# Coarse and fine exponents of an S4D unit in one product, with half of the coarse factors multiplied on GpSimd

## The chip, the cores and the metric

The kernel runs on one core of a Trainium2 chip. Its five engines have instruction streams of their own and meet through semaphores: PE (TensorE, matrix products into PSUM; PEld are its weight loads), DVE (VectorE), ACT (ScalarE, table functions and copies), POOL (GpSimd) and SP (SyncE, which issues nearly all DMAs here). The metric is the time of one execution on the device, in microseconds (us); lower is better.

## The reference

Two branches over the same length of 2048 positions and 640 channels are mixed by a gate:

```
dt = exp(log_dt);  A = -exp(log_A_real) + 1j*A_imag;  C = (C_real + 1j*C_imag) * dt
P = exp((A*dt)[:, :, None] * pos)                  # 640 channels x 128 states x 2048 positions
K = 2 * Re(einsum("dn,dnl->dl", C, P))             # taps: one filter of 2048 per channel
a = irfft(rfft(u, 4096) * rfft(K, 4096))[:2048] + u * D_skip
b = relu(x @ w1) @ w2                              # FFN, 640 -> 1728 -> 640
g = sigmoid((u * gate_w).sum(-1))
out = g * a + (1 - g) * b
```

The taps K are the part that the change touches. Position l is split into a coarse and a fine part, 64 coarse slots of 32 fine positions each. The complex exponential is then a product of a coarse and a fine factor, and the sum over the 128 states is a matrix product of the two.

## The kernel before

**Stages.** Three bodies of work are interleaved on the same engines. (1) The FFN: fp32 operands split into a high and a low part, three matmuls per product, in three passes over the hidden size (5, 5 and 4 blocks of 128). Its PSUM tile is pf. It has no dependence on the rest until the end, and fills PE wherever there is room. (2) The generation of the taps: 40 units of 16 channels (`products`, `factors`), joined in 20 pairs (`taps`). (3) The convolution by a two-stage transform, in 5 blocks of 128 channels (`conv`, PSUM tile pc). It opens when the last taps are in DRAM, since it reuses the memory of the generation.

**A unit.** `params` leaves eight rows per channel, high and low parts of the phase and magnitude parameters, in DRAM; `load_rows` fetches them as `R[c]`, 128 rows for 16 channels with the states along the columns. `products` (line 1166) multiplies them on PE by constant tables in `tg`. Two PSUM tiles result: pg, from four matmuls that each use a 32-row tile of PE (four channels, 512 columns: per channel 64 phases, 32 fine and 32 coarse, and 64 exponents of coarse factors), and pe, from one matmul over all 128 rows (16 channels x 32 exponents of fine factors). ACT rounds the phases to integers into sc (`whole`), takes the exponential of the coarse exponents into mg and of the fine ones into me (`exps`). DVE subtracts the integers from the phases (`part`, from PSUM and sc) and masks off the sign for the cosine. ACT takes sine and cosine of both.

**Factors.** `factors` (line 1213) makes, on DVE, the coarse sine factors G in two halves (the sine changes sign between the halves, which is why the 64 coarse slots stand in the order 32..63, 31..0, function `slots`), then mg times the cosine in place, then both fine factors times me. `taps` sums over the states on PE: 128 matmuls a unit pair and operand (mg and G against sc) into pk. DVE transposes pk to kt, POOL adds the skip term (an add of 128x8), and four DMAs store kt to kd. The convolution loads kd as ck.

**What sets the order.** Every piece of work is a task with an engine, an estimated duration, dependencies, buffer tokens from rings (pg, pe, pk have one buffer, mg four, sc five) and a rank. `Plan.run` plays the tasks against these estimates and emits the instructions engine by engine in the order in which it picks them. On the chip, each engine runs its stream in that fixed order. `moves` (line 135) adds a correction to the rank of single tasks by number. `Plan.add` with `port=True` charges a DVE task a quarter of the time in which POOL is taken by the estimates. All instructions are recorded through one helper, so the profile names one line for nearly all of them, and groups are told apart by tile names.

Short names used below: the subtraction is `sc<-pg,sc` on DVE, the masking `sc<-sc` on DVE, the cast `sc<-pg` on ACT, the exponential `mg<-pg` on ACT.

Of the kernel before, what the change touches and what calls it, by code (L numbers as in the profile page):

```python
# [46 lines left out]
TGR = 6  # L47
TGA = 4
# [26 lines left out]
def tables():  # L75
# [20 lines left out]
    tg = np.zeros((16, 8, 180))  # L96
    tg[:, :2, :32], tg[:, :2, 32:64], tg[:, 2:4, :32] = b, 32 * b + 16, 1
    tg[:, 4:6, 64:128], tg[:, 4:6, 128:160], tg[:, 6:, 128:160] = 32 * slots(), b, 1
    tg[np.arange(16), :, 160 + np.arange(16)] = 1
    tg[np.arange(16), :, 176 + np.arange(16) % 4] = 1  # L100
    f = lambda x: np.ascontiguousarray(x.astype(np.float32))
    return dict(t_g=f(tg.reshape(128, 180)), t_f1=f(np.tile(np.stack([f1, f1[slots()]], axis=1), (2, 1, 1))), t_w=f(w.reshape(128, 64)),
# [32 lines left out]
def moves():  # L135
    r = {}
    for v, s in (
# [318 lines left out]
class Kernel:  # L456
# [519 lines left out]
    def params(self):  # L976
# [116 lines left out]
        def steps_in():  # L1093
            tl['tgs'] = self.prm.tile([128, 180], F32, name="tgs")
            D_.dma_start(tl['tgs'], io['t_g'])
# [520 lines left out]
```

## Time and profile before

| | us |
|---|---|
| median of 3 runs (663.16 to 666.48) | 663.31 |
| profiled execution, its own time | 662.23 |
| span of that execution, first to last instruction | 660.5 |
| busy PE / DVE / ACT / POOL | 621.1 / 536.0 / 398.8 / 91.4 |

The span is cut into 40 slices of 16.5 us. Each digit of a slice is the busy share of an engine in tenths. Matmul records overlap in the pipe, so PE's busy share overstates how full it is; the distance between two starts says more. In the rows of groups, the columns are: operation, output<-inputs, shape, count | busy us, mean ns of one | idle time of the engine just before them and what ended it. In the rows of a timeline: start in us from the span's start, duration in us, engine, operation. A row of waits has the total, the count and the longest wait in us. The generation of taps lies between 87 us, when the first product of a unit runs, and 404 us, when the last pair is transposed; the convolution follows to the end.

### The profile page before, as it was taken

To read this page: it belongs to the slowest core of one execution; us is meant where nothing else is said; L and a number is where in the kernel's file an instruction comes from. 1 tells how busy PE (TensorE), PEld (TensorE's weight loads), DVE (VectorE), ACT (ScalarE), POOL (GpSimd) and SP (SyncE) were. 2 spreads that over 40 slices of the span, in tenths; PEclk is the share of its full clock that TensorE was granted. 3 is DMA by queue.
4 is the path that set the end of the run, shared out by engine and by line. 5 is a ranking of instruction groups with operands and counts; after the bars stand their busy time and mean duration, and the time that the engine had idled before them with its cause. 6 is when DMAs were issued, how large, how long until landed. Compare 5 with 4: busy or idle time off the path is not lost.

```text
span 660.5 us, 19174 instructions
## 1 busy us (share of the span) xinstructions
PE 621.1 (94%) x8236; PEld 486.3 (74%) x8236; DVE 536.0 (81%) x778; ACT 398.8 (60%) x591; POOL 91.4 (14%) x133
## 2 busy tenths in 40 slices
PE   7999999899999999999998998999888999998996
PEld 6999988797988978878876977655663445754666
DVE  4799939989999999988998994879568677977642
ACT  5447369999999888778798891032334342432631
POOL 0000000000000000000000000033051170612741
PEclk9999999999999999999998997999989999999999
DMA  9956675142555533425441363964515847336535
GB/s 243 328 190 195 195 221 176 25 162 81 171 169 187 211 121 122 169 97 192 150 119 39 109 165 123 331 191 82 212 39 151 199 124 161 130 100 168 144 104 129
DMA packets 76302, 102.79 MB, mean 156 GB/s; under 512 B 7609, under 2 KB 59449, under 8 KB 75962
## 3 DMA queue, kind: packets, MB, share of 16 engines
q1 hardware_dynamic: 76058, 101.16, 50.9%
q8 instruction: 65, 1.06, 0.7%
q10 hardware_dynamic: 160, 0.41, 0.2%
q14 instruction: 19, 0.16, 0.1%
HBM read 62.36 MB, written 39.19 MB: 154 GB/s over the span
## 4 chain that ended last, share of the span: by engine, by line
PE 66%; DVE 10%; issue 8%; DMA 6%; ACT 5%; SPq 2%; POOL 2%; POOLq 0%; DVEq 0%; ACTq 0%
PE pf L434 44%; PE pc L434 13%; PE pk L434 6%; PE pg L434 2%; DMA ck<-kd 2%; SPq L434 2%; DVE sc L434 2%; ACT sc L434 2%; DVE G L434 2%; DMA out_dram<-yo 2%; DMA xu<-in_A_u_dram 2%; PE pe L434 1%; POOL ku L434 1%; DVE mg L434 1%; ACT mg L434 1%
## 5 line engine op out<-in xcount | busy, mean ns | idle before, releaser
L434 PE MATMUL pf<-xx,w1h 128*128 128x256 f32 (+1 forms) x760 | 189.0, 346 | 1.5 <-DVE hl L434 0.9
L434 PEld LDWEIGHTS pf<-xx,w1h 128*128 128x128 f32 x760 | 125.1, 192 | 34.3 <-issue 21.1
L434 PE MATMUL pf<-xx,w1l 128*128 128x512 f32 (+1 forms) x340 | 116.5, 343 | 0.1
L434 DVE STREAM_TRANSPOSE ku<-pc 128x512 f32<-128x512 f32 x80 | 77.9, 1062 | 19.5 <-PE pc L434 19.4
L434 PE MATMUL pf<-w2h,hh 128*128 128x320 f32 x288 | 90.2, 317 | 2.5 <-DVE q L434 1.6
L434 PE MATMUL pf<-w2l,hh 128*128 128x320 f32 x288 | 88.1, 310 | 0.0
L434 ACT COPY ku<-pc 128x512 f32<-128x512 f32 (+1 forms) x60 | 43.8, 751 | 54.9 <-PE pc L434 54.9
L434 PE MATMUL pf<-w2h,hl 128*128 128x320 f32 x256 | 75.0, 317 | 0.0
L434 PEld LDWEIGHTS pf<-xx,w1l 128*128 128x128 f32 x340 | 65.1, 192 | 8.0 <-DVE w1l L434 0.3
L434 POOL TENSOR_TENSOR ku<-ku,kx 128x256 f32<-128x256 f32 x80 | 55.8, 735 | 97.8 <-DVE ku L434 34.9
L434 POOL TENSOR_TENSOR kt<-kt,dsk 128x8 f32<-128x8 f32 x20 | 8.4, 420 | 394.4 <-DVE kt L434 394.4
L434 ACT CAST sc<-pg 128x1024 int32<-128x1024 f32 x40 | 40.4, 1010 | 36.5 <-PE pg L434 36.5
L434 PEld LDWEIGHTS pf<-w2h,hh 128*128 128x128 f32 x288 | 54.3, 189 | 10.1 <-issue 4.9
L434 DVE TENSOR_TENSOR sc<-pg,sc 128x1024 f32<-128x1024 f32 x40 | 48.8, 1220 | 14.8 <-ACT mg L434 14.5
L434 PEld LDWEIGHTS pf<-w2l,hh 128*128 128x128 f32 x288 | 54.4, 189 | 0.2
L434 ACT ACT_TABLE_LOAD x42 | 53.9, 1283 | 0.7
L434 PEld LDWEIGHTS pf<-w2h,hl 128*128 128x128 f32 x256 | 46.5, 188 | 9.3 <-issue 9.3
L434 DVE TENSOR_TENSOR mg<-mg,sc 128x1024 f32<-128x1024 f32 x40 | 48.9, 1223 | 2.5
L434 DVE TENSOR_TENSOR sc<-sc,me 128x1024 f32<-128x1024 f32 x40 | 48.7, 1218 | 0.0
L434 ACT ACTIVATE hh<-pf 128x512 fp32r<-128x512 f32 (+1 forms) x40 | 20.4, 510 | 43.6 <-PE pf L434 43.4
L434 ACT ACTIVATE sc<-sc,half_pi 128x1024 f32<-128x1024 f32 x40 | 45.7, 1143 | 0.0
L434 PE MATMUL pk<-mg,sc 128*32 128x64 f32 x1280 | 39.8, 226 | 4.7 <-DVE sc L434 3.4
(166 smaller groups left out, 1197.2 us busy)
## 6 DMA issues: line engine op xcount, KB each, us to landing
xx<-xt SPq DMA_DIRECT2D x24, 640.0 KB, 7.7
xt<-xx SPq DMA_DIRECT2D x16, 640.0 KB, 6.3
part<-q SPq DMA_DIRECT2D x16, 640.0 KB, 3.3
q<-part SPq DMA_DIRECT2D x16, 640.0 KB, 4.6
ws<-in_B_w_dram SPq DMA_DIRECT2D x20, 320.0 KB, 3.5
kd<-kt SPq DMA_DIRECT2D x80, 64.0 KB, 1.7
ck<-kd SPq DMA_DIRECT2D x40, 128.0 KB, 3.6
xu<-in_A_u_dram SPq DMA_DIRECT2D x10, 512.0 KB, 7.7
```

The costliest lines, as they stand in the source:

```text
L434: return lambda *a, **k: self._tc.keep_in_program_order(f(*a, **k))
```

## The change

The fine exponents move into the 32-row tiles. Per channel a tile has 128 columns: 32 fine phases, 32 coarse phases, 32 coarse exponents (slots 32 down to 1) and 32 fine exponents. The matmul into pe is gone (the PSUM tile pe is left for the transposes at the start), and one exponential per unit covers coarse and fine exponents, 1024 elements a partition as the old coarse one did. It writes into a tile mg with 98 columns a channel. The upper 32 coarse factors are no longer exponentials: POOL multiplies the 32 computed ones, read backwards, by the factor of slot 31, into the first 32 columns, and sets the factor of slot 0 to 1. The factors on DVE read and write the same numbers of elements as before, at the new pitch. The table `t_g` shrinks from 180 to 132 columns and is scaled into `tg` by four ACT instructions in place of 20. The two halves of the coarse operand in `taps` stand apart in memory by 33 columns. The corrections in `moves` are replaced throughout, so that all five engines' orders are new.

```diff
-                q = st['pe', c] = self.psg.tile([128, 2, 256], F32, name="pe").rearrange("p a (d j) -> p (a d) j", j=32)
-                self.E.matmul(q.rearrange("p d j -> p (d j)"), R[c], self.tg[:, 512:], start=True, stop=True)
                 p = self.psg.tile([128, 8, 256], F32, name="pg").rearrange("p (r x) n -> p r (x n)", x=2)
                 for r in range(4):
                     x = slice(32 * r, 32 * r + 32)
-                    self.E.matmul(p[:, r], R[c][x], self.tg[x, :512], start=True, stop=True)
+                    self.E.matmul(p[:, r], R[c][x], self.tg[x], start=True, stop=True)
...
-            def exps(k):
-                def go():
-                    if k:
-                        st['mg', c] = st['gp'].tile([128, C, 64], F32, name="mg", bufs=4)
-                        S.activation(st['mg', c].rearrange("p (r e) j -> p r e j", e=4), st.pop(('px', c)), AF.Exp)
-                    else:
-                        st['me', c] = st['gp'].tile([128, C, 32], F32, name="me", bufs=4)
-                        S.activation(st['me', c], st.pop(('pe', c)), AF.Exp)
-                return go
+            def exps():
+                m = st['mg', c] = st['gp'].tile([128, C, 98], F32, name="mg", bufs=4)
+                S.activation(m[:, :, 32:].rearrange("p d (x j) -> p d x j", x=2)[:, :, :, :32], st.pop(('px', c)), AF.Exp)
+
+            def long():
+                m = st['mg', c]
+                P.memset(m[:, :, 64:65], 1.0)
+                P.tensor_mul(m[:, :, :32], m[:, :, 63:31:-1], m[:, :, 33:34].to_broadcast([128, C, 32]))
...
-            y = acts[c, 2] = A('ACT', None, 0.52, exps(0), [a, x], use=[e_, m_], rank=2, mode='exp')
-            d = A('DVE', 'g1', 1.14, part, [b, x], use=[p_, s_], rank=G1R)
+            d = A('DVE', 'g1', 1.14, lambda: V.tensor_sub(st['sc', c][0], st.pop(('pg', c)), I(st['sc', c][1])), [b, x],
+                  use=[p_, s_], rank=G1R)
+            y = A('POOL', 'm', 1.6, long, [x], use=[m_], rank=1)
...
-            tasks[c] = dict(s=s_, m=m_, exps=[x, y], trig=[sn, cs])
+            tasks[c] = dict(s=s_, m=m_, exps=[y, x], trig=[sn, cs])
...
-                        m = mg.rearrange("p d (h j) -> p d h j", h=2)
-                        V.tensor_mul(m, m, cs[:, :, None, 32:].to_broadcast([128, C, 2, 32]))
+                        V.tensor_mul(mg, mg, cs[:, :, None, 32:].to_broadcast([128, C, 2, 32]))
                     else:
                         x = st.pop(('s2', c))[:, :, :, :32]
-                        V.tensor_mul(x, x, me[:, None].to_broadcast([128, 2, C, 32]))
+                        V.tensor_mul(x, x, m[:, None, :, 65:97].to_broadcast([128, 2, C, 32]))
...
```

Left out of the diff are the two lists of `moves`, the host tables, the scaling of `tg`, views of the same tiles, and the list by which `ssm` puts ACT's tasks of a pair in line, which loses the second exponential.

More of the change, by code (lines that the diff above doesn't have):

```diff
@@ L93, in tables @@
             n[g % 4, :, g // 4, p, 1] = np.stack([sk, ck], axis=1)
[L96 to L100, printed above, removed]
+    tg = np.zeros((16, 8, 132))
+    tg[:, :2, :32], tg[:, :2, 32:64], tg[:, 2:4, :64] = b, 32 * b + 16, np.repeat([1, 0], 32)
+    tg[:, 4:6, 64:96], tg[:, 4:6, 96:128], tg[:, 6:, 96:128] = 32 * (32 - b), b, 1
+    tg[np.arange(16), :, 128 + np.arange(16) % 4] = 1
     f = lambda x: np.ascontiguousarray(x.astype(np.float32))
-    return dict(t_g=f(tg.reshape(128, 180)), t_f1=f(np.tile(np.stack([f1, f1[slots()]], axis=1), (2, 1, 1))), t_w=f(w.reshape(128, 64)),
+    return dict(t_g=f(tg.reshape(128, 132)), t_f1=f(np.tile(np.stack([f1, f1[slots()]], axis=1), (2, 1, 1))), t_w=f(w.reshape(128, 64)),
                 t_m=f(m.reshape(128, 32, 64)), t_n=f(n.reshape(128, 8, 2, 2, 64)))
@@ L1093, in steps_in @@
         def steps_in():
-            tl['tgs'] = self.prm.tile([128, 180], F32, name="tgs")
+            tl['tgs'] = self.prm.tile([128, 132], F32, name="tgs")
             D_.dma_start(tl['tgs'], io['t_g'])
@@ L1098, in go @@
             def go():
-                a, b = self.tg[:, :512].rearrange("p (x e j) -> p e x j", x=2, j=64), self.tg[:, 512:].rearrange("p (d j) -> p d j", j=32)
                 for d in ds:
-                    S.mul(b[:, d], tl['tgs'][:, 128:160], tl['tgs'][:, 160 + d:161 + d])
-                    if d % 4 == 0:
-                        S.mul(a[:, d // 4], tl['tgs'][:, :128].rearrange("p (x j) -> p x j", x=2),
-                              tl['tgs'][:, 176 + d // 4:177 + d // 4])
+                    S.mul(self.tg[:, d * 128:d * 128 + 128], tl['tgs'][:, :128], tl['tgs'][:, 128 + d:129 + d])
             return go
-        a = A('SP', 'tg', 0.62, steps_in, [self.prm0], kb=88, rank=TGR)
+        a = A('SP', 'tg', 0.62, steps_in, [self.prm0], kb=66, rank=TGR)
         if TGR > 5:
             self.late_loads.append(a)
-        for d in range(0, 16, 4):
-            self.tg_done.append(A('ACT', 'tg', 1.3, spread(range(d, d + 4)), [a], rank=TGA))
+        for d in range(0, 4, 2):
+            self.tg_done.append(A('ACT', 'tg', 0.7, spread(range(d, d + 2)), [a], rank=TGA))
         return [*done, *self.tg_done]
@@ L1123, in ssm @@
         self.gw = gk.tile([128, D], F32, name="gw")
-        self.tg = gk.tile([128, 1024], F32R, name="tg")
+        self.tg = gk.tile([128, 512], F32R, name="tg")
         dsk = gk.tile([128, n // 2, 2 * Q], F32, name="dsk")
@@ L1166, in products @@
         def products(c):
-            p_, e_, s_, m_ = tok('pg'), tok('pe'), tok('sc'), tok('mg')
+            p_, s_, m_ = tok('pg'), tok('sc'), tok('mg')
             rd, r_ = rows[c]
             def pe():
-                q = st['pe', c] = self.psg.tile([128, 2, 256], F32, name="pe").rearrange("p a (d j) -> p (a d) j", j=32)
-                self.E.matmul(q.rearrange("p d j -> p (d j)"), R[c], self.tg[:, 512:], start=True, stop=True)
                 p = self.psg.tile([128, 8, 256], F32, name="pg").rearrange("p (r x) n -> p r (x n)", x=2)
@@ L1175, in pe @@
                     x = slice(32 * r, 32 * r + 32)
-                    self.E.matmul(p[:, r], R[c][x], self.tg[x, :512], start=True, stop=True)
-                p = p.rearrange("p r (x e j) -> p x r e j", x=2, j=64)
-                st['pg', c], st['px', c] = p[:, 0], p[:, 1]
+                    self.E.matmul(p[:, r], R[c][x], self.tg[x], start=True, stop=True)
+                p = p.rearrange("p r (e j) -> p (r e) j", j=128)
+                st['pg', c], st['px', c] = p[:, :, :64], p[:, :, 64:].rearrange("p d (x j) -> p d x j", x=2)
             def whole():
@@ L1182, in whole @@
                 st['sc', c] = [st['s2', c][:, k] for k in range(2)]
-                S.copy(I(st['sc', c][1]).rearrange("p (r e) j -> p r e j", e=4), st['pg', c])
-            def exps(k):
-                def go():
-                    if k:
-                        st['mg', c] = st['gp'].tile([128, C, 64], F32, name="mg", bufs=4)
-                        S.activation(st['mg', c].rearrange("p (r e) j -> p r e j", e=4), st.pop(('px', c)), AF.Exp)
-                    else:
-                        st['me', c] = st['gp'].tile([128, C, 32], F32, name="me", bufs=4)
-                        S.activation(st['me', c], st.pop(('pe', c)), AF.Exp)
-                return go
@@ L1195, in part @@
-            def part():
-                x, y = (t.rearrange("p (r e) j -> p r e j", e=4) for t in st['sc', c])
-                V.tensor_sub(x, st.pop(('pg', c)), I(y))
-            a = visit[c] = A('PE', None, 0.5, pe, [rd, opened, *self.tg_done], take=[p_, e_], use=[r_], rank=GPR, mode='r', n=5)
+                S.copy(I(st['sc', c][1]), st['pg', c])
+            def exps():
+                m = st['mg', c] = st['gp'].tile([128, C, 98], F32, name="mg", bufs=4)
+                S.activation(m[:, :, 32:].rearrange("p d (x j) -> p d x j", x=2)[:, :, :, :32], st.pop(('px', c)), AF.Exp)
@@ L1199, in products @@
+            def long():
+                m = st['mg', c]
+                P.memset(m[:, :, 64:65], 1.0)
+                P.tensor_mul(m[:, :, :32], m[:, :, 63:31:-1], m[:, :, 33:34].to_broadcast([128, C, 32]))
+            a = visit[c] = A('PE', None, 0.24, pe, [rd, opened, *self.tg_done], take=[p_], use=[r_], rank=GPR, mode='r', n=4)
             b = acts[c, 0] = A('ACT', None, 0.97, whole, [a], take=[s_], use=[p_], rank=2)
-            x = acts[c, 1] = A('ACT', None, 0.96, exps(1), [a, b], take=[m_], use=[p_], rank=2, mode='exp')
@@ L1201, in products @@
-            y = acts[c, 2] = A('ACT', None, 0.52, exps(0), [a, x], use=[e_, m_], rank=2, mode='exp')
-            d = A('DVE', 'g1', 1.14, part, [b, x], use=[p_, s_], rank=G1R)
+            x = acts[c, 1] = A('ACT', None, 0.96, exps, [a, b], take=[m_], use=[p_], rank=2, mode='exp')
+            d = A('DVE', 'g1', 1.14, lambda: V.tensor_sub(st['sc', c][0], st.pop(('pg', c)), I(st['sc', c][1])), [b, x],
+                  use=[p_, s_], rank=G1R)
+            y = A('POOL', 'm', 1.6, long, [x], use=[m_], rank=1)
@@ L1205, in products @@
             h = TWO_PI
-            sn = acts[c, 3] = A('ACT', None, 1.0, lambda: S.activation(st['sc', c][0], st['sc', c][0], AF.Sin, scale=h), [o],
+            sn = acts[c, 2] = A('ACT', None, 1.0, lambda: S.activation(st['sc', c][0], st['sc', c][0], AF.Sin, scale=h), [o],
                   use=[s_], rank=2, mode='sin')
-            cs = acts[c, 4] = A('ACT', None, 1.06, lambda: S.activation(st['sc', c][1], st['sc', c][1], AF.Sin, scale=-h,
+            cs = acts[c, 3] = A('ACT', None, 1.06, lambda: S.activation(st['sc', c][1], st['sc', c][1], AF.Sin, scale=-h,
                                                           bias=self.half_pi), [o], use=[s_], rank=2, mode='sin')
-            tasks[c] = dict(s=s_, m=m_, exps=[x, y], trig=[sn, cs])
+            tasks[c] = dict(s=s_, m=m_, exps=[y, x], trig=[sn, cs])
         def factors(c):
@@ L1218, in go @@
                 def go():
-                    (sn, cs), mg, me = st['sc', c], st['mg', c], st['me', c]
+                    (sn, cs), m = st['sc', c], st['mg', c]
+                    mg = m[:, :, :66].rearrange("p d (h j) -> p d h j", h=2)[:, :, :, :32]
                     if k == 0:
                         G = st['G', c] = st['gp'].tile([128, C, 64], F32, name="G", bufs=2)
-                        V.scalar_tensor_tensor(G[:, :, :32], mg[:, :, :32], -1.0, sn[:, :, 32:], op0=ALU.mult,
+                        V.scalar_tensor_tensor(G[:, :, :32], mg[:, :, 0], -1.0, sn[:, :, 32:], op0=ALU.mult,
                                                op1=ALU.mult)
                     elif k == 1:
-                        V.tensor_mul(st['G', c][:, :, 32:], mg[:, :, 32:], sn[:, :, 32:])
+                        V.tensor_mul(st['G', c][:, :, 32:], mg[:, :, 1], sn[:, :, 32:])
                     elif k == 2:
-                        m = mg.rearrange("p d (h j) -> p d h j", h=2)
-                        V.tensor_mul(m, m, cs[:, :, None, 32:].to_broadcast([128, C, 2, 32]))
+                        V.tensor_mul(mg, mg, cs[:, :, None, 32:].to_broadcast([128, C, 2, 32]))
                     else:
                         x = st.pop(('s2', c))[:, :, :, :32]
-                        V.tensor_mul(x, x, me[:, None].to_broadcast([128, 2, C, 32]))
+                        V.tensor_mul(x, x, m[:, None, :, 65:97].to_broadcast([128, 2, C, 32]))
                 return go
@@ L1246, in pe @@
                 pk = st['pk'] = self.psg.tile([128, 2 * Q, 64], F32, name="pk")
-                x = [(*st.pop(('sc', c)), st.pop(('mg', c)), st.pop(('G', c))) for c in (2 * p, 2 * p + 1)]
+                x = [(*st.pop(('sc', c)), st.pop(('mg', c))[:, :, :66].rearrange("p d (h j) -> p d h j", h=2)[:, :, :, :32],
+                      st.pop(('G', c)).rearrange("p d (h j) -> p d h j", h=2)) for c in (2 * p, 2 * p + 1)]
                 for q in range(2 * Q):
@@ L1251, in pe @@
                             u, d = divmod(j * 2 * Q + q, C)
-                            self.E.matmul(pk[32 * j:32 * j + 32, q], x[u][1 - r][:, d, :32], x[u][2 + r][:, d],
+                            self.E.matmul(pk[32 * j:32 * j + 32, q].rearrange("p (h j) -> p h j", h=2), x[u][1 - r][:, d, :32], x[u][2 + r][:, d],
                                           start=r == 0, stop=r == 1)
@@ L1286, in ssm @@
             c = 2 * p
-            ks = [(c - 2, 3), (c - 2, 4), (c - 1, 3), (c - 1, 4), (c, 0), (c, 1), (c, 2), (c + 1, 0), (c + 1, 1), (c + 1, 2)]
+            ks = [(c - 2, 2), (c - 2, 3), (c - 1, 2), (c - 1, 3), (c, 0), (c, 1), (c + 1, 0), (c + 1, 1)]
             for k in ks:
```

235 rows, old and new, of the table r are left out of this document.

## The prediction

> **What bounds the kernel now.** I read the page first (busy shares, the slices, the chain), then a table by stage, then what the vector engine waited for inside the stage that the change touches.
>
> ```profile
> PE 621.1 (94%) x8236; PEld 486.3 (74%) x8236; DVE 536.0 (81%) x778; ACT 398.8 (60%) x591; POOL 91.4 (14%) x133
> PE   7999999899999999999998998999888999998996
> DVE  4799939989999999988998994879568677977642
> PE 66%; DVE 10%; issue 8%; DMA 6%; ACT 5%; SPq 2%; POOL 2%; POOLq 0%; DVEq 0%; ACTq 0%
> ```
>
> TensorE looks like the bound everywhere, and the chain agrees. But in slices 8 to 24 DVE is as full as PE. That is the generation of the taps (units, first at 91 us, last transposition at 404 us). The table by stage, columns PE, PEld, DVE, ACT, POOL busy in each stretch:
>
> ```profile
> 100.00:404.00 304.00, 290.95 (x4030) 248.43 (x4029) 283.54 (x382) 261.67 (x315) 8.19 (x19) 0.98 0.42 135
> 404.00:660.50 256.50, 236.86 (x3538) 149.01 (x3537) 177.99 (x245) 82.21 (x165) 82.30 (x107) 0.99 0.55 152
> ```
>
> DVE works 283.5 of 304.0 us in the generation and 178 of 256.5 in the convolution. PE's 291 is less full than it looks, because a matmul's record is longer than its place in the pipe: the rows below start every 0.15 us and last 0.31.
>
> ```profile
> 83.70 0.31 PE L434 MATMUL pf<-w2h,hh 128*128 128x320 f32 x1
> 83.85 0.31 PE L434 MATMUL pf<-w2l,hh 128*128 128x320 f32 x1
> ```
>
> So the generation has two bounds that lie close together, and DVE, whose records do not overlap like that, is the harder one. Its 20.5 us of idle time in the stretch are mostly these waits (total, times, longest):
>
> ```profile
> DVE sc L434 <- ACT mg L434: 5.2, 11, 1.0
> DVE G L434 <- ACT sc L434: 2.9, 8, 0.9
> DVE kt L434 <- PE pk L434: 2.7, 4, 1.0
> DVE xu L434 <- ACT xu L434: 2.0, 2, 1.6
> DVE kt L434 <- issue: 1.4, 2, 1.2
> DVE q L434 <- PE pf L434: 1.4, 4, 0.4
> ```
>
> They sum to 15.6 us. This is all that a faster PE or ACT can give back to DVE between 100 and 404 us.
>
> **PE: 40 products of the fine exponents go.** A unit's products in the pipe now:
>
> ```profile
> 234.95 0.39 PE L434 MATMUL pf<-xx,w1l 128*128 128x512 f32 x1
> 235.18 0.40 PE L434 MATMUL pe<-tg,PS 128*128 128x512 f32 x1
> 235.51 0.50 PE L434 MATMUL pg<-tg,PS 32*128 32x512 f32 x4
> 235.94 0.73 PE L434 MATMUL pf<-xx,w1h 128*128 128x512 f32 x2
> ```
>
> The product into pe holds the pipe from 235.18 to 235.51, 0.33 us, against 0.23 for the same shape just ahead of it (234.95 to 235.18). The change from whole columns to 32-row tiles stays, now behind an FFN matmul, so I take 0.23 x 40 = 9.2 us; the upper bound is 0.33 x 40 = 13.2. The four pg matmuls keep their size. This is PE time in a stage where DVE is fuller, so it only counts through what it lets other work do.
>
> **ACT: 40 fine exponentials go, and 16 of the 20 scalings that build tg.**
>
> ```profile
> L434 ACT ACTIVATE me<-pe 128x512 f32<-128x512 f32 x40 | 24.2, 606 | 0.0
> ```
>
> 24.2 us leave an engine that works 262 of 304. The fine exponential stood between a unit's coarse one and what ACT does next, so sines and casts come up to 0.6 us sooner. The tg scalings lie at 46 to 52 us, ahead of any unit: nothing.
>
> These two parts take work out from in front of four of the six waits above. Of the 15.6 us I take 9 back (rather more than half; bounds 0 and 15.6): the waits on ACT and on pk shrink, those on the FFN's own matmuls less.
>
> **POOL: 40 x (a memset of 128x16, a product of 128x512).** Nearest rows, with the three DVE instructions whose layout changes:
>
> ```profile
> L434 POOL TENSOR_TENSOR yo<-yo,yj 128x512 f32<-128x512 f32 x8 | 10.3, 1289 | 31.1 <-ACT yo L434 16.9 <-issue 14.3
> masks.py:197 POOL MEMSET ident<- 128x128 f32 x1 | 0.2, 204 | 0.3 <-POOLq L1605 0.3
> L434 DVE TENSOR_TENSOR mg<-mg,sc 128x1024 f32<-128x1024 f32 x40 | 48.9, 1223 | 2.5
> L434 DVE TENSOR_TENSOR sc<-sc,me 128x1024 f32<-128x1024 f32 x40 | 48.7, 1218 | 0.0
> L434 DVE TENSOR_TENSOR sc<-pg,sc 128x1024 f32<-128x1024 f32 x40 | 48.8, 1220 | 14.8 <-ACT mg L434 14.5
> ```
>
> Some 1.4 us a unit, 56 us in all, on an engine that is busy 8 of 304. DVE's count stays the same, and a pitch of 98 costs it nothing: the op on sc and me writes half-filled blocks and takes 1218 ns, as the dense one on mg does with 1223. The added wait is that G and mg of a unit need POOL's product and not just the exponential. Behind them on DVE stand the rest of the unit and then pk on PE. It is covered: after the exponential come the subtraction, the masking and two sines.
>
> ```profile
> 297.89 1.04 ACT L434 ACTIVATE mg<-pg 128x1024 f32<-128x1024 f32 x1
> 298.96 1.23 DVE L434 TENSOR_TENSOR sc<-pg,sc 128x1024 f32<-128x1024 f32 x1 [0.23 <-ACT mg L434]
> 301.82 0.69 DVE L434 SCALAR_TENSOR_TENSOR G<-mg,sc 128x512 f32<-128x512 f32 x1 [0.90 <-ACT sc L434]
> ```
>
> The exponential is ready at 298.93 and the product by 300.4; the next G on DVE, at 301.82, is that of the pair's first unit, and this unit's own reader comes later still. Without that cover it would cost at most 1.4 us a unit. The 20 small additions to kt queue behind these products on POOL; only the stores of kd wait for them, and behind the last pair no product is left: nothing.
>
> **The cost of that part is DVE's.** POOL and DVE get in each other's way in this stage already:
>
> ```profile
> 228.60 0.65 DVE L434 SCALAR_TENSOR_TENSOR G<-mg,sc 128x512 f32<-128x512 f32 x1
> 228.75 0.57 POOL L434 TENSOR_TENSOR kt<-kt,dsk 128x8 f32<-128x8 f32 x1 [15.29 <-DVE kt L434]
> 316.25 0.21 POOL L434 TENSOR_TENSOR kt<-kt,dsk 128x8 f32<-128x8 f32 x1 [19.52 <-DVE kt L434]
> L434 POOL TENSOR_TENSOR kt<-kt,dsk x20: 208/566/697, 115.0 to 404.0; 128x8 f32<-128x8 f32 x20
> ```
>
> An addition of 0.21 us takes 0.57 where DVE is in an op on two SBUF tensors, and ends with it (229.25 against 229.32). The other direction, DVE held by a POOL op of 1.29 us, no row shows. Bounds: nothing, and every product in full, 40 x 1.29 = 52 us. The value is nearer the lower end, because of the place: the product can start when the exponential ends, and there DVE stands at the subtraction from PSUM (0.03 us behind the exponential in the rows above), 1.22 us long, with one operand in SBUF. What sticks out is 1.29 + 0.10 (half of the memset row) - 1.22 = 0.17 us, 7 us over 40 units. I take +7.
>
> The Trainium skill, "SBUF — State Buffer", section "Who interferes with whom", states that a DVE instruction with two SBUF inputs contends with a GpSimd instruction that reads SBUF, that whoever starts first keeps the pair for its whole instruction, and that a DVE instruction with at most one SBUF input does not contend. The 0.57 us row agrees for one direction; by this rule the other one exists too, which speaks against the change, and the subtraction is free of it. By the rule the sum moves up with each unit in which POOL is not served beside the subtraction, as the third rival has it.
>
> **The ranks.** All orders are new; the built programs show three things. First, 19 fewer FFN matmuls of 320 columns stand ahead of the first unit, 19 x 0.147 = 2.8 us.
>
> ```profile
> 86.78 0.31 PE L434 MATMUL pf<-w2l,hh 128*128 128x320 f32 x1
> 86.93 0.40 PE L434 MATMUL pe<-tg,PS 128*128 128x512 f32 x1
> 91.53 1.23 DVE L434 TENSOR_TENSOR sc<-pg,sc 128x1024 f32<-128x1024 f32 x1 [9.07 <-ACT mg L434]
> 81.61 1.04 SPq L434 DMA_DIRECT2D PS<-ps  x2
> PS<-ps SPq DMA_DIRECT2D x10, 256.0 KB, 3.6
> ```
>
> DVE stands idle for 9 us until the first unit, so this counts; the rows of the first units land at 81.6 + 3.6 = 85.2, which leaves 1.7 of it, and their load moves ahead of two loads of xu on SP. I take -2 (bounds 0 and -2.8). Second, the DVE work ahead of the last transposition of taps is the same to within 1 us by the rows of its groups. Third, 12 more FFN matmuls of 320 columns stand ahead of the first one of the convolution: 12 x 0.147 = 1.8 us that the freed PE does while DVE is the bound. The convolution, where PE is 92% busy, is shorter by as much: -1.8.
>
> **Sum.** -2 - 9 + 7 - 1.8 = -5.8 us. The profiled execution took 662.23 us (span 660.5 and 1.7 around it), 1.1 under the median of 663.31. It would go to 656.4, the median to 657.5.
>
> **Rivals.** (1) PE is the bound after all: the pipe's 13 us and the 2.8 at the start come through, no DVE time is lost: 663.3 - 16 - 1.8 = 645.5. The chain (PE 66%) speaks for it, DVE's 283.5 of 304 against. (2) The change doesn't help: DVE is the bound so firmly that only 2 us of its waits come back; -2 - 2 + 7 - 1.8 = +1.2, 664.5. For it: six waits spread over 31 places, none over 1.6 us; a static order returns such pieces badly. (3) Slower: the product isn't served beside the subtraction, but just before, when DVE is behind. It then holds up an op on two SBUF tensors for up to 1.29 us, DVE falls further behind, and the next product meets it again. At half of the units this is 26 us in place of 7: +13, 676.5. It decides from 13 us of hold on, 0.32 us a unit. For it: DVE has 20 us of slack and ACT gets ahead by 0.6 us a unit; against: pg is one buffer, so a unit's exponential cannot run before the last subtraction is done. (4) The new order leaves 40 FFN matmuls in place of 96 behind the last convolution matmul, 56 x 0.147 = 8.2 us less to fill the last block's chain of copies and stores; if the chain leaves PE dry earlier by that, +8.2 - 5.8 = +2.4, 665.7.
>
> **Chances.** Forecast 0.33, rival (1) 0.15, (2) 0.2, (3) 0.2, (4) 0.12. A measurement of this kernel can tell about 0.5%, 3.3 us, from no change. Faster: the forecast and (1), 0.48. Slower: (3), and most of (4) and some of (2) where they come out a little worse, 0.3. Within: the rest, 0.22. The range reaches from (1) to most of (3), 646 to 674; the forecast alone has 651 to 660.
>
> **What would show it.** Right: POOL's product at about 1.3 us in the records, mostly beside the subtraction; the first subtraction near 89.5 us; DVE busy in the generation unchanged, its waits on ACT at some 3 us; the last transposition near 398 us; PE with more idle time there. Wrong: gaps of about 1 us in front of DVE's masking or mg ops while POOL runs (rival 3), a POOL product well over 1.4 us, a last transposition at 404 or later (2), DVE waits falling to near nothing with the convolution much earlier (1), or PE idle after 600 us (4).

## The result and the profile after

The changed kernel takes 671.69 us (median of 4 runs, 670.82 to 673.07), against 664.47 us for the kernel before (4 runs, 663.16 to 666.48): a ratio of 1.0108, 95% interval 1.0072 to 1.0143. It is 1.1% slower where the prediction said 1% faster. The profiled execution took 671.55 us, its span is 669.8.

From the page of the changed kernel, the span and the busy times:

```profile
span 669.8 us, 19196 instructions
...
PE 613.2 (92%) x8196; PEld 481.6 (72%) x8196; DVE 535.4 (80%) x778; ACT 376.8 (56%) x535; POOL 148.0 (22%) x213
```

PE has lost 7.9 us of records and 40 matmuls, ACT 22 us, POOL has gained 57, DVE is unchanged. This is as foreseen, and yet the span is 9.3 us longer. The generation, by the table by stage and by DVE's waits in it:

```profile
100.00:404.00 304.00, 286.89 (x4022) 247.93 (x4022) 284.62 (x381) 242.99 (x278) 62.07 (x94) 0.98 0.43 138
```

```profile
DVE kt L416 <- PE pk L416: 8.1, 10, 2.3
DVE hl L416 <- ACT hh L416: 3.1, 2, 1.7
DVE w1l L416 <- ACT w1h L416: 1.4, 2, 1.2
DVE sc L416 <- ACT mg L416: 0.9, 3, 0.4
DVE q L416 <- PE pf L416: 0.5, 1, 0.5
DVE G L416 <- ACT sc L416: 0.2, 1, 0.2
```

The waits on ACT before the subtraction fell from 5.2 to 0.9 us and those before G from 2.9 to 0.2, as the lighter ACT promised. But kt now waits 8.1 us for the taps in place of 2.7, and others came up: 14.2 us in all, against 15.6. The operations by their groups, and then the marks of both ends of the convolution, in the changed kernel and in the one before (a row for a tile gives min/median/max in ns, then the first and the last start; kt is the transposition of taps, tw the last product of each block):

```profile
L416 POOL TENSOR_TENSOR mg<-mg 128x512 f32<-128x512 f32 x40 | 51.9, 1298 | 177.1 <-ACT mg L416 177.1
L416 DVE TENSOR_TENSOR mg<-mg,sc 128x1024 f32<-128x1024 f32 x40 | 50.5, 1262 | 2.3
```

```profile
L416 DVE STREAM_TRANSPOSE kt<-pk x20: 702/716/718, 113.7 to 408.2; 128x512 f32<-128x512 f32 x20
L416 PE MATMUL pc<-ku,tw x80: 589/590/646, 494.0 to 655.1; 128*64 128x512 f32 x80
```

```profile
L434 DVE STREAM_TRANSPOSE kt<-pk x20: 705/711/718, 114.1 to 403.3; 128x512 f32<-128x512 f32 x20
L434 PE MATMUL pc<-ku,tw x80: 589/590/646, 494.4 to 640.6; 128*64 128x512 f32 x80
```

The last transposition comes 4.9 us late, at 408.2. By the first tw product both kernels are level again (494.0 and 494.4): slack in the first block took it up. The last tw product starts 14.5 us later than before. The end of the program, by the chain of the changed kernel and then of the kernel before (start, duration, what):

```profile
637.89 4.06 DMA y__84<-yo
642.01 3.10 DMA ws<-y__84
...
647.10 4.96 PE pf L416 x32
652.06 1.74 PE pc L416 x7
653.80 0.53 ACT yo L416 x2
...
656.43 2.49 DMA out_dram<-yo
...
659.02 0.64 ACT yo L416 x3
```

```profile
637.63 3.59 PE pc L434 x16
641.22 7.24 PE pf L434 x48
648.49 0.56 DVE q L434
```

Before, the chain runs through PE: the last pc products, then FFN matmuls, and the sums behind them. After, it ends in the last block's copy, sum, store and the next copy, which waits for the store to give its buffer back. The FFN matmuls behind the last tw product, by a table of the tile pf alone, in the kernel before and in the changed one (behind the stretch and its length stands PE's busy time with its count):

```profile
641.20:660.50 19.30, 14.29 (x96) 14.03 (x96) 4.41 (x8) 0.00 (x0) 0.92 0.54 123
```

```profile
655.60:669.80 14.20, 6.12 (x40) 5.85 (x40) 2.20 (x4) 0.00 (x0) 0.86 0.54 120
```

These matmuls run without a gap. PE's last one is therefore over at 655.5 us before (641.20 + 14.29) and at 661.7 after (655.60 + 6.12); what still follows takes 5.0 us before and 8.1 after. So of the 9.3 us, 3.1 are the tail that the fourth rival foresaw, and 6.2 have been lost ahead of PE's last matmul. What the causes are, the experiments have to say.

### The profile page after: what moved, and what is told of

The parts are those of the page before. It is cut to its first block, busy times and chain, and to the rows that moved or that the text cites. A ratio compares the mean times of both kernels' runs of the same rounds, so it can differ in the third digit from the quotient of the medians.

```text
span 669.8 us, 19196 instructions
## 1 busy us (share of the span) xinstructions
PE 613.2 (92%) x8196; PEld 481.6 (72%) x8196; DVE 535.4 (80%) x778; ACT 376.8 (56%) x535; POOL 148.0 (22%) x213
## 4 chain that ended last, share of the span: by engine, by line
PE 50%; DVE 20%; issue 11%; ACT 7%; DMA 6%; SPq 2%; POOL 2%; POOLq 0%; DVEq 0%; ACTq 0%
PE pf L416 33%; PE pc L416 10%; PE pk L416 5%; DVE sc L416 5%; ACT sc L416 3%; DVE G L416 3%; SPq L416 2%; PE pg L416 2%; DMA y__84<-yo 2%; DVE mg L416 2%; DVE ku L416 2%; DMA xu<-in_A_u_dram 2%; ACT mg L416 1%; POOL ku L416 1%; DVE hl L416 1%
## 5 line engine op out<-in xcount | busy, mean ns | idle before, releaser
L416 POOL TENSOR_TENSOR mg<-mg 128x512 f32<-128x512 f32 x40 | 51.9, 1298 | 177.1 <-ACT mg L416 177.1
L416 DVE STREAM_TRANSPOSE ku<-pc 128x512 f32<-128x512 f32 x80 | 76.1, 1061 | 6.3 <-PE pc L416 6.2
L416 DVE TENSOR_TENSOR sc<-pg,sc 128x1024 f32<-128x1024 f32 x40 | 48.7, 1217 | 9.6 <-ACT mg L416 9.3
L416 ACT ACT_TABLE_LOAD x42 | 53.9, 1283 | 2.7 <-PE pk L416 2.0
L416 DVE TENSOR_TENSOR mg<-mg,sc 128x1024 f32<-128x1024 f32 x40 | 50.5, 1262 | 2.3
L416 DVE TENSOR_TENSOR sc<-sc,mg 128x1024 f32<-128x1024 f32 x40 | 49.5, 1238 | 0.0
L416 PE MATMUL pc<-ku,tm 64*32 64x256 f32 x1280 | 43.4, 397 | 6.4 <-issue 4.2
L416 DVE STREAM_TRANSPOSE ku<-ku 128x512 f32<-128x512 f32 x40 | 25.5, 685 | 25.9 <-ACT ku L416 25.9
```

The costliest lines, as they stand in the source:

```text
L416: return lambda *a, **k: self._tc.keep_in_program_order(f(*a, **k))
```

## The experiments

**The tool: code and order apart.** A changed rank moves everything behind it, so ranks cannot be taken back one by one. In all kernels below the planner is therefore replaced by a recorded list, in which the tasks are emitted:

```diff
     def run(self):
-        self.free = {e: 0.0 for e in self.LAG}
-        ...
+        for n in ORDER.split():
+            self.tasks[int(n)].fn()
```

The changed kernel's own list gives its own five streams. "Old" and "new" below are the lists of the kernel before and of the changed one, with tasks matched by their role. A list spliced at a task has one order up to that task, and then all tasks still missing in the relative order of the other.

### Code against order

```diff
 x1: changed code,  ORDER = old (POOL's product right behind its exponential)
 x2: code before,   ORDER = new
```

> The changed code (one product, one exponential, POOL's multiplication), emitted in the exact order in which the kernel before emits its tasks; the POOL product follows its exponential. Theory (the new orders cost the time, the code itself gains a little): 656 to 663, faster than before by up to 1%, the last transposition of taps at 400 or earlier. Rival A (POOL holds DVE up): 668 to 676, with DVE's mg and sc ops over 1.35 us in the mean. Rival B (the changed code is worth nothing either way): 663 to 666.

> The code before (the product into pe, two exponentials, no product on POOL), emitted in the exact order of the changed kernel. Theory (the new orders cost it): 672 to 680, as slow as the changed kernel or slower, with relay 4 of the convolution at 650 or later. Rival A (POOL holds DVE up): 660 to 666. Rival B (code worth nothing): 671 to 673.

x1: 662.10 us, ratio 0.9990 (0.9956 to 1.0023). x2: 668.91, ratio 1.0074 (1.0039 to 1.0110). The new order makes even the old code slower by 0.7%; the new code in the old order is worth nothing that can be measured. So the order is the loss. (x2 came out between its ranges: less slow than the theory and rival B had it, slower than rival A.) The theory's second half, a small gain of the code, did not show, which left a question: is the code without effect, or do two effects cancel?

### The two terms of the code

```diff
 y3: changed code, ORDER = old
-                P.tensor_mul(m[:, :, :32], m[:, :, 63:31:-1], m[:, :, 33:34].to_broadcast([128, C, 32]))
+                P.memset(m[:, :, :32], 1.0)
 y4: changed code, ORDER = old
+                q = self.psg.tile([128, 512], F32, name="pe")
+                self.E.matmul(q, R[c], self.tg, start=True, stop=True)
```

> The changed code in the order of the kernel before throughout, but POOL fills the upper 32 coarse factors with ones in place of the product (that part of the taps is left out, so the output is another one); POOL then reads nothing there. If POOL's product holds DVE or delays G: 655 to 660, at least 2 us under the 662.1 with the product, and the last transposition earlier than 404.2. If it costs nothing: 660 to 664, last transposition 403 to 405.

> The changed code in the order of the kernel before throughout, with one more matmul of 128x512 per unit, into the free tile pe, which nobody reads: the product that the change took away from PE. If PE's freed time reaches the end: 666 to 674 (40 x 0.32 = 13 us). If DVE bounds the generation and PE's freed time is idle: 660 to 665, and a mean granted clock nearer to that of the kernel before (0.986) than to 0.979.

y3: 656.59 us, ratio 0.9909 (0.9872 to 0.9947). y4: 670.10, ratio 1.0092 (1.0064 to 1.0119). They cancel. Against x1, PE's product is worth 1.0% (6.8 us) and POOL's costs 0.8% (5.4 us). The last transposition moves along, in x1, y3 and y4 in this order:

```profile
L437 DVE STREAM_TRANSPOSE kt<-pk x20: 703/713/718, 113.7 to 403.5; 128x512 f32<-128x512 f32 x20
L437 DVE TENSOR_TENSOR mg<-mg,sc 128x1024 f32<-128x1024 f32 x40 | 51.1, 1278 | 2.5
L437 DVE TENSOR_TENSOR sc<-sc,mg 128x1024 f32<-128x1024 f32 x40 | 50.4, 1259 | 0.0
L437 POOL TENSOR_TENSOR mg<-mg 128x512 f32<-128x512 f32 x40 | 51.3, 1283 | 203.0 <-ACT mg L437 193.9 <-PE pf L437 6.2 <-DMA xx<-xt 2.9
```

```profile
L437 DVE STREAM_TRANSPOSE kt<-pk x20: 706/713/718, 113.3 to 398.9; 128x512 f32<-128x512 f32 x20
L437 DVE TENSOR_TENSOR mg<-mg,sc 128x1024 f32<-128x1024 f32 x40 | 48.9, 1223 | 2.5
L437 DVE TENSOR_TENSOR sc<-sc,mg 128x1024 f32<-128x1024 f32 x40 | 48.7, 1217 | 0.0
```

```profile
L437 DVE STREAM_TRANSPOSE kt<-pk x20: 704/710/718, 113.4 to 407.7; 128x512 f32<-128x512 f32 x20
```

403.5 becomes 398.9 without POOL's product and 407.7 with PE's. My idea that PE's freed time lies idle because DVE is the bound has fallen: 4.2 us of it reach the end of the generation. POOL's price is seen in DVE's records: the two rows above are 2.2 and 1.7 us longer in x1. It is not spread evenly. Six of these 80 operations last 1.5 to 2.1 us, which makes up these 3.9 us; one of them in x1:

```profile
176.04 1.05 POOL L437 TENSOR_TENSOR mg<-mg 128x512 f32<-128x512 f32 x1 [4.62 <-ACT mg L437]
176.10 2.06 DVE L437 TENSOR_TENSOR sc<-sc,mg 128x1024 f32<-128x1024 f32 x1
```

DVE was late, POOL's product started 0.06 us ahead of an operation with both operands in SBUF, and this took 2.06 us in place of 1.22.

### Where in the order

```diff
 x3: changed code, ORDER = new, from the opening of the convolution on old
 x4: changed code, ORDER = old, from the opening of the convolution on new
 y1: changed code, ORDER = new, from block 2's first tn product on old
 y2: changed code, ORDER = old, from block 2's first tn product on new
```

> The changed kernel in its own order up to the opening of the convolution; everything still to come from there in the relative order of the kernel before. Theory (the loss comes from the new order of the convolution's last blocks): 660 to 666, since the opening is 5 us later but both kernels stood level at 499 us. If the loss came from the late opening: 669 to 673. Rival A has no say on the part behind the opening: 669 to 673 too.

> The changed code in the order of the kernel before up to the opening of the convolution, then the changed kernel's own order for all that is still to come. Theory (the new order of the last blocks costs it): 668 to 674. If the late opening costs it: 660 to 666.

> The changed kernel in its own order up to the first inverse product of the convolution's block 2 (tile tn, about 537 us), then all that is still to come in the relative order of the kernel before. Theory (the new order of the last two blocks costs it): 660 to 666, tn4 within 4 us of the end of tm4. If the loss lies in the order ahead of that point: 668 to 673.

> The changed code in the order of the kernel before up to the first inverse product of block 2, then the changed kernel's order. Theory (last two blocks): 667 to 673, with some 12 us between the end of tm4 and the start of tn4. If the loss lies ahead of that point: 660 to 664, as in the old order throughout (662.1).

x3: 665.53 us, 1.0073 (1.0034 to 1.0113). x4: 669.40, 1.0131 (1.0079 to 1.0183). y1: 662.30, 0.9989 (0.9952 to 1.0026). y2: 672.83, 1.0139 (1.0097 to 1.0180). With the new order up to some 537 us nothing is lost; with it from there on everything is. The late opening costs nothing by y1, although x3, which switches earlier, lies 0.7% up; its runs spread from 662 to 671, and why it is worse than y1 I cannot say.

```diff
 z1: changed code, ORDER = old, from block 4's first tm product on new
 z2: changed code, ORDER = old, from block 3's last relay on new
 w1: changed code, ORDER = new, from block 4's first tm product on old
```

> The changed code in the order of the kernel before up to the first spectral product of the convolution's last block (tile tm, about 610 us), then the changed kernel's order. Three of four tw products of block 3 lie ahead of that point, so only the place of the last one and of tn4 behind some 10 us of FFN matmuls, and the 40 in place of 96 FFN matmuls behind the last pc matmul, are new. If tn4's place behind the FFN alone costs it: 667 to 673. If the late relays of block 3 cost it: 661 to 664.

> The same with the changed kernel's order from the last relay of block 3 on (about 589 us): relays of block 3 in one go, as in the kernel before, but its four tw products behind block 4's tm products, and tn4 behind the FFN, as in the changed kernel. If the split relays alone cost it: 661 to 664. If the late tw and tn cost it: 668 to 673, as with the new order from block 2 (672.8).

> The changed kernel in its own order up to the first tm product of the last block, the order of the kernel before from there, so that 96 FFN matmuls follow the last pc matmul again. If the end alone costs it: 661 to 665, level with the kernel before. If the split relays and late tw products ahead of that point cost something of their own: 666 to 670.

z1: 668.14 us, 1.0094 (1.0052 to 1.0137). z2: 666.88, 1.0056 (1.0024 to 1.0087). w1: 673.13, 1.0158 (1.0121 to 1.0195). By z1 the stretch behind tm4 costs 0.9% by itself. z2, which switches earlier, shows no more (0.6%, between its two ranges). w1 was a miss: the old order behind that point did not mend it. A splice late in the program makes a mixture of its own (in w1 the last tm products take 18 us in place of 10), so I went over to moves of single groups of tasks.

```diff
 v1: changed code, ORDER = old; the last block's tn, relays, tw, copies, sums and stores
     (tasks 1212-1247) moved to behind the FFN tasks that the new order has ahead of them
 v2: changed code, ORDER = new; block 3's last four relays, its tw products, copies, sums
     and stores (tasks 1130-1133, 1146-1163) moved to where the old order has them
```

> The changed code in the order of the kernel before, with one thing moved: the last block's tn products, relays, tw products, copies and stores stand where the changed kernel has them, so that 12 instead of 2 groups of four FFN matmuls come between the last tm and the first tn product and 40 instead of 96 matmuls follow the last pc matmul. If this alone costs the time: 667 to 673 (662.1 without it, and up to 56 x 0.147 = 8.2 us more). If it is hidden: 661 to 664.

> The changed kernel in its own order, but block 3's last four relays, its tw products, copies, sums and stores stand where the kernel before has them, ahead of block 4's tm products. If their late place costs it: 662 to 667. If the last block's place costs it: 669 to 673.

v1: 672.73 us, 1.0125 (1.0067 to 1.0184). v2: 675.89, 1.0166 (1.0122 to 1.0209). One move, in an order that is otherwise the old one, costs 1.35% against x1, 8.9 us, as much as the whole loss. The reverse, this one move taken back in the new order, was not run. The marks and the end of the chain in v1:

```profile
L437 PE MATMUL pc<-ku,tw x80: 589/590/646, 494.6 to 655.8; 128*64 128x512 f32 x80
```

```profile
652.79 1.74 PE pc L437 x7
654.53 0.53 ACT yo L437 x2
...
658.51 2.49 DMA out_dram<-yo
...
661.11 0.13 ACT yo L437
```

It is the chain of the changed kernel. In x1 the last tw products are over at 642.5, and the chain ends in the 96 FFN matmuls that still follow:

```profile
638.92 3.59 PE pc L437 x16
642.52 14.28 PE pf L437 x96
...
656.89 0.55 DVE q L437
```

But this chain is the smaller part of the 8.9 us. In x1 PE's last matmul is over at 656.8 (642.52 + 14.28), 5.0 us before the end of the span of 661.8; in v1 at 662.4 (the second row below), 8.1 us before the end of its 670.5. The traces agree on this: 8.0 to 8.1 us in all nine with 40 matmuls behind the last tw product, 4.9 to 5.3 us in all nine with 96, w1 among them. So leaving the end uncovered costs some 3 us. The other 5.7 us of v1 are lost ahead of PE's last matmul. Most of it can be seen among the FFN matmuls that the move puts between the last tm and the first tn product:

```profile
629.27 1.22 PE L437 MATMUL pf<-xx,w1h 128*128 128x512 f32 x2 [3.05 <-DVE hl L437]
662.14 0.31 PE L437 MATMUL pf<-w2h,w2l 128*128 128x320 f32 x1
```

PE stands for 3.05 us, since these matmuls wait for DVE's hl (which waits for ACT's hh, and ACT had stood 5.26 us for the load of q from part), and then two of them take 1.22 us in place of 0.61: the granted clock is 0.50 from 628.5 to 635.0. Moved FFN work is no free filler. This is one trace; that all four runs of v1 have a mean clock of 0.970 to 0.976, and x1's ten 0.979 in the mean, fits it.

v2 also clears a suspect that the chain had named: block 3's late store and the load that waits for it (y__84 and ws in the chain of the changed kernel). Put back early, it gains nothing; the kernel is slower still, slower than either range had it.

### The product beside the subtraction

If POOL's price is the chance meeting with an operation on two SBUF tensors, it goes when POOL waits until DVE has done its last such operation ahead of the subtraction.

```diff
 c1: changed code, ORDER = old;  c2: the order of y1;  w2: ORDER = new
     (POOL's task stands right ahead of its unit's subtraction in the list)
                 P.memset(m[:, :, 64:65], 1.0)
+                if 'last' in st:
+                    P.tensor_sub(m[:, :, 97:98], st['last'], st['last'])
                 P.tensor_mul(m[:, :, :32], ...)
...
                         V.tensor_mul(mg, mg, cs[:, :, None, 32:].to_broadcast([128, C, 2, 32]))
+                        st['last'] = m[:, :, :1]
...
                         V.tensor_mul(x, x, m[:, None, :, 65:97].to_broadcast([128, 2, C, 32]))
+                        st['last'] = x[:, 0, :, :1]
```

> The changed code in the order of the kernel before, with POOL's product held until DVE has done its last mg or sc multiplication ahead of the unit's subtraction (a small POOL subtraction into an unused column reads its result), so that it runs beside the subtraction, which reads PSUM. If the 4.4 us by which DVE's mg, sc and G ops were longer than without the product are contention with it: 656 to 659, mean of the mg op back at 1.23 us, last transposition near 400. If the product costs by being late for G: 662 or more.

> The same hold of POOL's product, in the changed kernel's order up to block 2's inverse product and the order of the kernel before from there (662.3 without the hold). If contention is what the product costs: 656 to 660. If not: 661 to 664.

> The changed kernel in its own order throughout, with POOL's product held back to run beside the subtraction. If POOL's hold of DVE is part of the 1.1%: 665 to 668. If the new order hides it, since the generation's end waits for FFN matmuls and not for DVE: 669 to 673, with DVE's mg op at 1.22 us all the same.

c1: 657.00 us, 0.9922 (0.9886 to 0.9958). c2: 662.45, 0.9987 (0.9964 to 1.0010). w2: 668.56, 1.0104 (1.0050 to 1.0157). From the groups of c1, the marks of its taps, and the place of the long operation shown above:

```profile
L437 DVE TENSOR_TENSOR mg<-mg,sc 128x1024 f32<-128x1024 f32 x40 | 48.9, 1222 | 2.5
L437 DVE TENSOR_TENSOR sc<-sc,mg 128x1024 f32<-128x1024 f32 x40 | 48.6, 1216 | 0.0
L437 POOL TENSOR_TENSOR mg<-mg 128x512 f32<-128x512 f32 x40 | 41.9, 1049 | 25.7 <-ACT mg L437 25.4 <-DMA xx<-xt 0.4
L437 DVE STREAM_TRANSPOSE kt<-pk x20: 702/716/718, 114.2 to 401.2; 128x512 f32<-128x512 f32 x20
```

```profile
175.62 1.22 DVE L437 TENSOR_TENSOR sc<-sc,mg 128x1024 f32<-128x1024 f32 x1
176.75 1.22 DVE L437 TENSOR_TENSOR sc<-pg,sc 128x1024 f32<-128x1024 f32 x1
176.92 0.23 POOL L437 TENSOR_TENSOR mg<-sc 128x16 f32<-128x16 f32 x1 [5.18 <-DVE sc L437]
177.09 1.05 POOL L437 TENSOR_TENSOR mg<-mg 128x512 f32<-128x512 f32 x1
```

Both sides are freed: DVE's means are those of y3, and POOL's product falls from 1283 to 1049 ns. The kernel is 0.8% faster than the one before and 1.8% faster than the changed one: the version that beats both. In the new order the same hold shows no gain (c2 against y1, w2 against the changed kernel: the ratios differ by 0.02 and 0.04%), though DVE's mg operations are back at 1223 ns in w2. So contention is not shown to be a part of the 1.1%; w2 lies between its two ranges, and its interval leaves room for half a per cent. The interval of c1 leaves open how much of POOL's 0.8% it recovers; its last transposition, at 401.2, has 2.3 of the 4.6 us.

## Why the prediction was wrong

- **The failed step is the third point on the ranks, -1.8 us.** It counted 12 more FFN matmuls ahead of the convolution as a gain, and took the convolution as a stage that PE bounds from end to end. The new order also puts FFN work ahead of the last block, and v1 shows what that costs: +8.9 us. The prediction had this move as its fourth rival, gave it a chance of 0.12 and set it against a gain of 5.8, so that it came out at +2.4. That both built programs already showed 40 in place of 96 matmuls made it a fact of the order, not a chance. Its size (56 x 0.147 = 8.2 us) comes near the measured 8.9 by luck: the mechanism named, an end that the FFN no longer covers, is worth some 3 us. The rest is lost ahead of PE's last matmul, in v1 mostly where PE waits for DVE's hl and then has half the clock, and the prediction has no term for that. In the changed kernel 6.2 us are lost there; its trace shows PE standing for 4.16 us ahead of a tm product at 561.9, and the clock at 0.50 from 562.1 to 565.5, but no run ties this to the move of v1, so that the cause of this part stays open.
- **Waits given back, -9: the size was off by a quarter to a third, the way to it was wrong.** PE's product is worth 6.8 us (y4); y3, which has PE's and ACT's part and no product on POOL, lies 6.0 us below the kernel before. ACT's part was not run by itself. I reasoned through DVE's waits, and in x1 little of them came back: the waits for G fell, those of kt for pk rose. In the changed kernel the waits went from 15.6 to 14.2 us, and the last transposition came at 408.2 us, where the prediction had it near 398. That the gain comes through the taps' matmuls, which stand behind the FFN on PE, is only argued.
- **POOL's hold of DVE, +7: 5.4 (y3).** The mechanism was right in the main and its form was not. The subtraction is free of it (1217 ns in the mean, most of the 40 beside POOL's product). But the price is no 0.17 us that stick out of every unit: it is a few meetings of 0.3 to 0.85 us, as the third rival had it, at six operations in place of half of all units. The rule named there (Trainium skill, "SBUF — State Buffer", "Who interferes with whom": the order of issue decides who blocks) is what the 2.06 us row shows, and by y3 a POOL instruction that only writes does not hold DVE.
- **Start of the units, -2.** The first subtraction came at 89.91 in place of 91.53, 1.6 us. In x1, with the old order, it starts at 91.74: the gain belonged to the order, and it was lost again before 404 us.

```profile
89.91 1.23 DVE L416 TENSOR_TENSOR sc<-pg,sc 128x1024 f32<-128x1024 f32 x1 [6.58 <-ACT mg L416]
```

- **The sum for the code alone**, without the terms of the ranks, was -9 + 7 = -2. Measured: -6.8 + 5.4 = -1.4 from its two parts, -0.7 as a whole (x1, within its interval of -2.9 to +1.5).

## What to carry to other kernels

When a change comes with a new order, replay each order with each code before judging either: here the code was worth nothing that could be measured, and one move in the order cost as much as the whole loss. Keep enough matmuls behind the last dependent product to cover its copies and stores (some 3 us here); the chain tells by whether it ends in PE rows or in copy, store, copy. Then look at the place that the moved matmuls went to: here they waited for another engine. An operation given to POOL is best tied to a stretch in which DVE reads PSUM, not merely issued as early as it can be: in the old order this gained 0.7% (the intervals of c1 and x1 just touch), in the new one nothing that could be measured.

## What the runs showed that was not expected

The granted clock falls to one half, in stretches of 3.41 us or twice that, after a short lull of PE, which need not be a standstill. Four stretches of the kernel before (columns as in the tables above; the clock is the third number from the right):

```profile
353.69:357.10 3.41, 1.46 (x9) 0.95 (x9) 3.27 (x4) 1.66 (x3) 0.00 (x0) 1.00 0.00 0
357.10:360.50 3.40, 3.40 (x37) 2.71 (x37) 3.40 (x5) 3.20 (x4) 0.00 (x0) 0.50 0.02 5
394.69:398.10 3.41, 0.83 (x7) 0.27 (x5) 3.31 (x4) 3.27 (x6) 0.00 (x0) 1.00 1.00 178
398.10:404.93 6.83, 5.40 (x128) 4.91 (x129) 4.67 (x7) 0.42 (x1) 0.21 (x1) 0.50 0.02 6
```

PE was busy for 1.46 and 0.83 of 3.41 us, and the next stretch ran at half the clock. The Trainium skill, "TensorE: Matmul & The Clock Gate", section "What's actually happening", gives an idle window of about 3.4 us as the condition; the length agrees, but here a window that is a quarter to two fifths busy was enough. The mean clock was 0.986 over 25 runs of the kernel before and 0.979 over 10 of x1, 0.7% of 660 us or 4.6 us of clock, and 0.987 for the old code in the new order. Most runs of the new code are low (means of 0.974 to 0.982), which may be a part of why it gains so little. But y1 and c2, new code too, have 0.984, so it is not the code alone. Nor is it just the freed PE time, for with the product put back (y4) it is 0.979 too. What lowers it stays open.
